# Side casts ahead of the sums' casts, an earlier rest for the weights' pieces, and two moved groups of transfers in a gated mix of linear and softmax attention

## The chip, the cores and the metric

The kernel runs on one core of a Trainium2 chip. The metric is the device time of one execution in microseconds. The kernel before took 2826.58 us as the median of three runs (2825.94 to 2827.85). The profiled execution, from which every row below comes, took 2824.52 us, 2.06 us under that median; its span of instructions is 2822.7 us.

## The reference

One token matrix `x` (2048 tokens, width 1024, fp32) goes through two attention blocks, and a gate mixes their outputs:

```python
x = A_x
g = _sigmoid((x * gate_w).sum(-1, keepdims=True))
a = _A_ref(x, A_wqkv, A_wo)     # linear attention, 32 heads of 32
b = _B_ref(x, B_wqkv, B_wo)     # softmax attention, 32 heads of 32
return g * a + (1 - g) * b

# in A: phi = lambda t: jnp.where(t > 0, t + 1, jnp.exp(t)) + 1e-6
#       o = phi(q) @ (phi(k)^T v) / (phi(q) @ sum(phi(k)) + 1e-6), then o @ wo
# in B: p = softmax(q k^T / sqrt(32)), then (p v) @ wo
```

## The kernel before

**Arithmetic.** [...] Where the result has to be near fp32, an operand is kept as two parts: `split` (line 293) makes `hi`, a ScalarE cast of the source, and `lo`, the source minus `hi`, on VectorE. `three` issues three matmuls for one product of such operands (lines 153, 156 and 158: hi with hi, hi with lo, lo with hi).

**Stages.** The program has one order for each engine, written out by hand (`manual_schedule`), and every engine works through its own order, waiting on semaphores.

1. A pass over the first half of the tokens for the values V (`v_pass(0, ...)`), to about 50 us of the span.
2. Eight *quads* of the first half (J=0). A quad makes two blocks of Q or K columns by a Strassen-like scheme with seven products instead of eight. `quad` runs `product(0)` to `product(6)`, 12 matmuls each, into the eight PSUM banks in turn (`bank[next(turns) % NQB]`). VectorE adds the products (the sums `C11`, `P1`, `W2`, `U2`), and `store` splits each finished sum and sends both parts to DRAM (`qk`).
3. `v_pass(1, ...)` for the second half: for each of eight steps it starts with all eight banks in order, so at its first step it needs every bank that the last quad used.
4. Eight quads of the second half (J=1), to about 415 us.
5. The long rest, from about 415 to 2675 us: linear attention (`linear`), the maxima of the softmax scores (`maxima`) and the heads (`heads_`) interleaved by a planner in the program (`T`, `use`, `behind`), which fixes the order when the program is built. Then the output product.

**Side work.** A quad has a generator `side`; each `next(side)` issues one step. `quad_weights` makes the seven weight operands of the next quad in six steps: adds and subtractions on VectorE, and splits (`part`) into a ring of 13 slots. The operand with number 2 is made in step 5 and is needed by the third product of the next quad. Also in `side`: `spill` stores the split x to DRAM, `reload_wv` loads V's weights again for the second half (transfers `big<-wv`), `change` (in the last quad of the first half) splits x of the second half, and `wo_parts` makes the operands of the output weights. The last runs on GpSimd: a piece is a cast, subtractions and transfers on GpSimd's own queue; a tiny ScalarE copy (line 511, `dn<-eps`) lets each piece start, and 28 pieces are spread over the steps of both halves.

**Transfers.** Nearly all transfers are issued by SyncE (line 170), in order. An issue also waits until the transfer eight issues earlier, which used the same semaphore, has landed.

**The long rest.** `load_half` loads half of a token's x (or of A's attention output) for `linear`; `store_mix` stores two or more small blocks of a mixed weight (`wa`). When a head's maxima are complete, `rows` turns them into a row, split into `mh` and `ml` (16 x 128 each), and four transfers write these into two extra rows of the head's query operand: token tiles 0 to 3 go to `q_first`, tiles 4 to 15 to `q_rest`. The matmul of line 1382 (scores of the head) reads `q_first` for j = 0 and `q_rest` for the others.

Of the kernel before, what the change touches and what calls it, by code (L numbers as in the profile page):

```python
# [3 lines left out]

# [16 lines left out]
DH = 32  # L21
C = 512
# [16 lines left out]
WARM = 8  # L39
NE = 3  # L40
AHEAD_X = 3
PIECE_STEP = 3.4
GATE_STEP, GATE_FROM = 2.3, 20.0
LATE = 1.0
MANUAL = {ET.PE, ET.DVE, ET.Activation, ET.SP, ET.Pool}
# [4 lines left out]
def kernel(  # L50
# [18 lines left out]
    nc = tc.nc  # L69
# [3 lines left out]
    HK = NK // 2  # L73
    NT = S // P
    NJ = S // C
    TPC = C // P
# [5 lines left out]
    def f32(ap):  # L82
        return ap.bitcast(F32)

    def f32r(ap):
        return ap.bitcast(F32R)
# [30 lines left out]
    mh = sb.tile([NT, P], F32R, name="mh")  # L117
    ml = sb.tile([NT, P], F32R, name="ml")
# [16 lines left out]
    q_first, q_rest = [big[0][:, :C], big[2][:, :C], None], [big[0], big[2]]  # L135
# [153 lines left out]
    def raw_tile(n):  # L289
        nraw[0] += 1  # L290
        return raws[nraw[0] % n]

    def split(hi, lo, src, eng):
        nc.scalar.copy(hi, src)  # L294
        eng.tensor_sub(lo, src, f32(hi))  # L295

    def load_cols(w, cols, k, n):

# [121 lines left out]
    def quad_weights(raws, J, f):  # L420

        w11, w12, w21, w22 = raws

        def part(s, raw):
            n = quad_ring(J, f, s)
            split(ring_w(n, 0), ring_w(n, 1), raw, nc.vector)

        part(0, w11)
        part(6, w22)
        nc.vector.tensor_add(w22, w21, w22)  # L430
        yield
        nc.vector.tensor_sub(w21, w11, w21)
        part(1, w12)
        yield
        nc.vector.tensor_sub(w11, w22, w11)
        part(3, w22)
        yield
        nc.vector.tensor_sub(w12, w12, w11)
        part(4, w11)
        yield  # L440
        part(2, w12)
        yield
        part(5, w21)
# [3 lines left out]
    def quad(J, f, side):  # L447

        sec, g = quad_cols(f)

        def product(s):
            ps = bank[next(turns) % NQB]
            n = quad_ring(J, f, s)
            for i in range(KH):
                sl = slice(i * P, (i + 1) * P)
                stat = [ring_w(n, p)[:, sl] for p in range(2)]
                for _ in three(ps, stat, [xpiece(J, PRODUCTS[s], p, i) for p in range(2)], i, n=KH):
                    pass
            return ps

        def store(i, jj, src, hi):
            split(f32r(hi), f32r(src), src, nc.vector)
            j = 2 * J + jj
            for p, part in enumerate((hi, src)):
                dma(qk_d[sec][p][g + i][:, j * C:(j + 1) * C], part)

        nc.scalar.copy(P1, product(0))
        next(side, None)
        nc.vector.tensor_add(C11, product(1), P1)
        store(0, 0, C11, H11)  # L470
        next(side, None)
        p3 = product(2)
        next(side, None)
        p5 = product(3)
        next(side, None)
        nc.vector.tensor_add(U2, product(4), P1)
        nc.vector.tensor_add(W2, p5, U2)
        nc.vector.tensor_add(P1, p3, W2)
        store(0, 1, P1, H12)
        next(side, None)  # L480
        p7 = product(5)
        nc.vector.tensor_add(W2, p7, W2)
        nc.vector.tensor_add(U2, p7, U2)
        store(1, 1, W2, H22)
        next(side, None)
        nc.vector.tensor_add(U2, product(6), U2)  # L486
        store(1, 0, U2, H21)
        next(side, None)

    def wo_piece(m, i):  # L490
        half, l = int(m[1]) - 1, int(m[2]) - 1
# [164 lines left out]
    def load_pair(raws, J, i):  # L656
        for k in (2 * i, 2 * i + 1):
            for jj in range(2):
                load_x(raws, J, jj, k)

    def quads(J, first, *others):

        sides_ = [late_side(J), *others]
        for f in range(QUADS - 1):
            if f + 2 < QUADS:
                load_quad(raws_q[f % 2], f + 2)
            else:
                first()
            quad(J, f, beside(quad_weights(raws_q[(f + 1) % 2], J, f + 1), *sides_))

    def spill_rest(J):
        part = 0
        for name in ("X11", "X21", "X22"):
            for _ in spill(J, name):
                part += 1
                for _ in range(2 if part % 4 else 1):
                    yield
# [50 lines left out]
        split_x(raw_x1[1], 1, 1, 3)  # L728
        yield

    quads(0, lambda: load_pair(raw_x1[0], 1, 0), reload_wv(), spill_rest(0), parts)
    load_pair(raw_x1[1], 1, 1)
    quad(0, QUADS - 1, change())
    for k in range(NK):
# [306 lines left out]
    def linear():  # L1041
        extra = iter(())
        for n, (i, t) in enumerate(units):
# [18 lines left out]
            for k in range(NK):  # L1062
                yield lambda: ended(w_left[k], w_ready[k], xp_ready.get(2 * n + k // HK, 0.0))
                need(w_left[k])
                if n < TPC:
                    stat = [xpiece(1, xname(0, k % 2), p, k // 2)[:, t * P:(t + 1) * P] for p in range(2)]
                else:
                    stat = [xstat_lin(n, k, p) for p in range(2)]
                for m, _ in enumerate(three(ps, stat, (wpart(k, 0), wpart(k, 1)), k)):
                    lin_pe(1.0)  # L1070
                    if m < 2:
                        yield always
                store_mix()
                if kind == "v":
                    if n in (4, 5) and k == 0:
                        load_v(n - 4)
                if n == 1 and k == 0:
                    for m in range(2 * TPC, 2 * TPC + 3):
                        load_half(m)
                if k % HK == HK - 1 and 2 * n + k // HK >= 2 * TPC:  # L1080
                    load_half(2 * n + k // HK + 3)
# [166 lines left out]
    def rows(h):  # L1248
        m = mneg
        end = use("dve", 0.14)  # L1250
        nc.vector.tensor_reduce(m, mx[h % 2], AX.X, ALU.max, negate=True)

        def turn():
            b = take()
            pm = bank[b]
            end = use("pe", 0.12, free[b])
            nc.tensor.transpose(pm[:NT, :P], m, ident)
            end = use("act", 0.2, end)
            nc.scalar.copy(mh, pm[:NT, :P])

            def low(end):
                rows_ready[h] = end + 2.5
                nc.vector.tensor_sub(ml, pm[:NT, :P], f32(mh))
                for i, part in enumerate((mh, ml)):
                    r = 3 * DH + i
                    for q, ts in ((q_first[h % 3], slice(0, TPC)), (q_rest[h % 2][:, C:], slice(TPC, NT))):
                        dma(f32(q[r:r + 1, :]).rearrange("o (t c) -> o t c", c=P), f32(part[ts]))

            give(b, 0.0, [defer(low, end, 0.2, 0)])

        tasks.append((lambda: both(bank_at(), end), turn))
# [654 lines left out]
```

## Time and profile before

| | |
|---|---|
| median of 3 runs | 2826.58 us |
| profiled execution, its time | 2824.52 us |
| its span of instructions | 2822.7 us |
| TensorE busy | 2801.9 us, 99% |
| VectorE busy | 2330.5 us, 83% |
| GpSimd busy | 2104.1 us, 75% |
| ScalarE busy | 1638.2 us, 58% |
| moved by transfers | 459.52 MB, mean 163 GB/s |

A row of a group or of the order of time names the line, the engine, the operation, what it writes and reads (`out<-in`, buffer numbers left out), the shape and the count; in brackets stands the idle time of the engine before it and what ended that. PE is TensorE, DVE VectorE, ACT ScalarE, POOL GpSimd, SP SyncE. A table of windows gives busy time (and count) of each engine in each stretch, TensorE's granted clock (PEclk), the busy share of the transfer engines and what they moved.

### The profile page before, as it was taken

The numbers are of one execution on the slowest core, as the hardware profiler recorded it, in microseconds if no ns is written. First come the engines' busy times: TensorE is split into PE (matmuls) and PEld (weight loads), VectorE is DVE, ScalarE is ACT, GpSimd is POOL, SyncE is SP. The second block draws the span as 40 slices with busy tenths as digits, with TensorE's granted clock in tenths as the row PEclk, the third lists the DMA queues.
The fourth block names the chain that finished last, engine by engine and source line by source line (L and its number), as shares of the span: only waits on it lengthen the run. The fifth ranks groups of instructions, "written<-read, shape, count | busy, mean of one in ns | idle before, by whom it ended". The sixth has DMA issues, their size and how long they took to land.

```text
span 2822.7 us, 47003 instructions
## 1 busy us (share of the span) xinstructions
PE 2801.9 (99%) x15880; PEld 2043.3 (72%) x15880; DVE 2330.5 (83%) x3745; ACT 1638.2 (58%) x3095; POOL 2104.1 (75%) x1150
## 2 busy tenths in 40 slices
PE   9999999999999999999999999999999999999999
PEld 8877887777767776677766777776676667666687
DVE  7887865888878888888888888888877888886688
ACT  5334332566666666666766666676666666666522
POOL 0651433699999999999899988989889988888000
PEclk9999999999999999999999999999999999999999
DMA  8997979533343434333433444456575555544774
GB/s 279 301 335 224 293 224 282 175 100 102 103 127 97 106 98 131 94 98 102 126 105 96 106 131 129 151 167 186 172 213 159 145 158 146 145 121 140 255 238 152
DMA packets 403340, 459.52 MB, mean 163 GB/s; under 512 B 106894, under 2 KB 234894, under 8 KB 401308
## 3 DMA queue, kind: packets, MB, share of 16 engines
q1 hardware_dynamic: 381084, 419.03, 47.5%
q0 software_dynamic: 22016, 37.50, 6.2%
q8 instruction: 126, 2.06, 0.3%
q14 instruction: 114, 0.93, 0.1%
HBM read 314.31 MB, written 127.66 MB: 157 GB/s over the span
## 4 chain that ended last, share of the span: by engine, by line
PE 90%; DMA 2%; issue 1%; DVE 0%; ACT 0%; SPq 0%; ACTq 0%; DVEq 0%
PE bank L1382 17%; PE bank L1240 16%; PE bank L1532 16%; PE bank L153 13%; PE bank L156 13%; PE bank L158 13%; PE bank L1304 1%; PE bank L1026 1%; PE bank L915 0%; DMA big<-ra 0%; DMA xh<-xs 0%; SPq L170 0%; PE bank L1296 0%; DMA qk<-mid 0%; DVE big L295 0%
## 5 line engine op out<-in xcount | busy, mean ns | idle before, releaser
L1467 POOL TENSOR_TENSOR big<-big,big 128x512 f32<-128x512 f32 (+2 forms) x694 | 1641.7, 2369 | 107.5 <-ACT big L1385 64.4
L1245 DVE TENSOR_REDUCE mx<-bank 128x1 f32<-128x512 f32 x2048 | 1313.5, 682 | 305.9 <-PE bank L1240 301.9
L1385 ACT ACTIVATE big<-bank 128x512 f32<-128x512 f32 x2048 | 1179.6, 602 | 433.7 <-PE bank L1382 368.4
L1382 PE MATMUL bank<-big,big 128*128 128x512 f32 x1888 | 742.4, 394 | 2.2 <-DMA big<-ml 2.2
L1240 PE MATMUL bank<-big,big 128*128 128x512 f32 x1888 | 739.8, 392 | 1.1 <-ACT big L1385 1.1
L153 PE MATMUL bank<-big,big 128*128 128x512 f32 x1576 | 618.1, 392 | 9.2 <-DVE mid L486 3.9
L158 PE MATMUL bank<-big,big 128*128 128x512 f32 x1572 | 614.9, 391 | 0.5 <-DMA big<-xs 0.2
L156 PE MATMUL bank<-big,big 128*128 128x512 f32 x1576 | 615.4, 390 | 0.0
L1532 PE MATMUL bank<-big,mid 128*32 128x512 f32 x4096 | 454.2, 593 | 0.0
L1382 PEld LDWEIGHTS bank<-big,big 128*128 128x128 f32 x1888 | 354.5, 188 | 127.3 <-issue 48.1
L1240 PEld LDWEIGHTS bank<-big,big 128*128 128x128 f32 x1888 | 355.0, 188 | 75.0 <-ACT big L1385 2.4
L153 PEld LDWEIGHTS bank<-big,big 128*128 128x128 f32 x1576 | 296.9, 188 | 77.6 <-ACT big L294 4.5
L158 PEld LDWEIGHTS bank<-big,big 128*128 128x128 f32 x1572 | 295.8, 188 | 65.9 <-DVE big L295 3.0
L156 PEld LDWEIGHTS bank<-big,big 128*128 128x128 f32 x1576 | 296.7, 188 | 61.3 <-DVE big L295 0.2
L1532 PEld LDWEIGHTS bank<-big,mid 128*32 128x32 f32 x4096 | 143.9, 110 | 264.1 <-issue 263.8
L1483 DVE TENSOR_TENSOR bank<-bank,big 128x512 f32<-128x512 f32 x364 | 251.5, 691 | 5.3 <-ACT big L1385 2.9
L295 DVE TENSOR_TENSOR big<-mid,big 128x512 fp32r<-128x512 f32 (+1 forms) x157 | 122.2, 795 | 44.6 <-ACT big L294 44.2
L294 ACT CAST big<-mid 128x512 fp32r<-128x512 f32 (+1 forms) x157 | 92.8, 618 | 113.1 <-DVE mid L1651 66.0
L1463 POOL TENSOR_TENSOR big<-big,big 128x1536 f32<-128x1536 f32 (+1 forms) x31 | 122.9, 3964 | 44.8 <-ACT big L1385 44.8
L153 PE MATMUL bank<-big,xh 128*128 128x512 f32 x376 | 147.1, 391 | 2.4 <-DMA xh<-xs 2.4
L158 PE MATMUL bank<-big,xh 128*128 128x512 f32 x376 | 146.9, 391 | 0.0
L156 PE MATMUL bank<-big,xh 128*128 128x512 f32 x376 | 146.8, 390 | 0.0
(163 smaller groups left out, 2123.0 us busy)
## 6 DMA issues: line engine op xcount, KB each, us to landing
big<-xs SPq DMA_DIRECT2D x288, 256.0 KB
big<-qk SPq DMA_DIRECT2D x690, 64.0 KB
xh<-xs SPq DMA_DIRECT2D x144, 256.0 KB
qk<-mid SPq DMA_DIRECT2D x128, 256.0 KB
big<-oA SPq DMA_DIRECT2D x84, 256.0 KB
xs<-big SPq DMA_DIRECT2D x64, 256.0 KB
oA<-mid SPq DMA_DIRECT2D x64, 256.0 KB
big<-big POOLq DMA_DIRECT2D x50, 256.0 KB, 5.4
```

The costliest lines, as they stand in the source:

```text
L153: yield nc.tensor.matmul(ps, sh, mh_, start=(kt == 0), stop=False)
L156: yield nc.tensor.matmul(ps, sh, ml_, start=False, stop=(late and last))
L158: yield nc.tensor.matmul(ps, sl, mh_, start=False, stop=last)
L295: eng.tensor_sub(lo, src, f32(hi))
L1240: nc.tensor.matmul(bank[b], q[:, t % TPC * P:(t % TPC + 1) * P], k[:, j * C:(j + 1) * C], start=True, stop=True)
L1245: nc.vector.tensor_reduce(m[:, t, j:j + 1], bank[b], AX.X, ALU.max)
L1382: nc.tensor.matmul(bank[b], k[:, t * P:(t + 1) * P], q_cols(h, j), start=True, stop=True)
L1385: nc.scalar.activation(pr_t[i][:, j * C:(j + 1) * C], bank[b], AF.Exp, scale=SCALE)
L1463: nc.gpsimd.tensor_add(lacc[:, :qp], pr(0)[:, :qp], pr(1)[:, :qp])
L1467: nc.gpsimd.tensor_add(lacc[:, sl], lacc[:, sl], pr(t)[:, sl])
L1483: nc.vector.tensor_add(lacc[:, qp:] if t == NT - 1 else l_b[:, :n], l_b[:, :n], src)
L1532: nc.tensor.matmul(av_b[j * DH:(j + 1) * DH, :], v[:, t, :], pr(t)[:, j * C:(j + 1) * C], start=(t == 0), stop=(t == NT - 1))
```

## The change

Four edits.

1. **Order in a quad.** `split` hands its VectorE part to `vec`. While `kept[0]` is a list, `vec` only notes the instruction. `step` runs one side step in that state: its ScalarE casts, GpSimd work and transfers are issued at once, its VectorE instructions are returned. `store` now issues the sum's cast, then the noted VectorE instructions, then the sum's subtraction. So in three places of a quad the side's casts stand ahead of the sum's cast on ScalarE, and the side's VectorE part stands between the sum and the sum's subtraction. The step that stood behind the store of `W2` is noted and issued only behind the last sum's addition (`U2 += product(6)`). Transfers of a side step (spills, reloads) now stand ahead of the sum's stores on SyncE.
2. **Rest of the pieces.** In the first half, `parts` advances for six quads (42 steps) instead of seven (49). In the order of instructions this makes 16 pieces in the first half and 12 in the second, where it was 19 and 9.
3. **`load_half` ahead of `store_mix`** in `linear`: x is issued before two blocks of `wa` instead of after them.
4. **Maxima's rows** go tile group by tile group: `mh` and `ml` of `q_first`, then `mh` and `ml` of `q_rest`; it was `mh` of both, then `ml` of both.

```diff
+    def vec(fn, *args):
+        if kept[0] is None:
+            fn(*args)
+        else:
+            kept[0].append((fn, args))
     def split(hi, lo, src, eng):
         nc.scalar.copy(hi, src)
-        eng.tensor_sub(lo, src, f32(hi))
+        if eng is nc.vector:
+            vec(eng.tensor_sub, lo, src, f32(hi))
+        else:
+            eng.tensor_sub(lo, src, f32(hi))
...
-        def store(i, jj, src, hi):
-            split(f32r(hi), f32r(src), src, nc.vector)
+        def step():
+            ops = kept[0] = []
+            next(side, None)
+            kept[0] = None
+            return ops
+
+        def store(i, jj, src, hi, ops=()):
+            nc.scalar.copy(f32r(hi), src)
+            for fn, args in ops:
+                fn(*args)
+            nc.vector.tensor_sub(f32r(src), src, hi)
...
-        store(0, 1, P1, H12)
-        next(side, None)
+        store(0, 1, P1, H12, ops)
         p7 = product(5)
+        ops = step()
         nc.vector.tensor_add(W2, p7, W2)
         nc.vector.tensor_add(U2, p7, U2)
         store(1, 1, W2, H22)
+        p4 = product(6)
         next(side, None)
-        nc.vector.tensor_add(U2, product(6), U2)
-        store(1, 0, U2, H21)
-        next(side, None)
+        nc.vector.tensor_add(U2, p4, U2)
+        store(1, 0, U2, H21, ops)
...
-    quads(0, lambda: load_pair(raw_x1[0], 1, 0), reload_wv(), spill_rest(0), parts)
+    quads(0, lambda: load_pair(raw_x1[0], 1, 0), reload_wv(), spill_rest(0), islice(parts, (QUADS - PIECE_REST) * NP))
...
+                if k % HK == HK - 1 and 2 * n + k // HK >= 2 * TPC:
+                    load_half(2 * n + k // HK + 3)
                 store_mix()
...
-                for i, part in enumerate((mh, ml)):
-                    r = 3 * DH + i
-                    for q, ts in ((q_first[h % 3], slice(0, TPC)), (q_rest[h % 2][:, C:], slice(TPC, NT))):
+                for q, ts in ((q_first[h % 3], slice(0, TPC)), (q_rest[h % 2][:, C:], slice(TPC, NT))):
+                    for i, part in enumerate((mh, ml)):
+                        r = 3 * DH + i
```

The order on TensorE and on GpSimd is the same in both kernels, instruction for instruction (line numbers aside).

**VectorE in the last quad of the first half**, from the first sum that reads `product(4)` (`bank_243`). `mid_234` is `U2`, `mid_235` `W2`, `mid_226` `P1`; `mid_231` to `mid_233` are the casts of the sums; `mid_224` to `mid_228` hold x of the second half, whose splits are the side work. Before:

```order
L476 TENSOR_TENSOR mid_234<-bank_243,mid_226 128x512
L477 TENSOR_TENSOR mid_235<-bank_242,mid_234 128x512
L478 TENSOR_TENSOR mid_226<-bank_241,mid_235 128x512
L295 TENSOR_TENSOR mid_226<-mid_226,mid_232 128x512
L295 TENSOR_TENSOR big_213<-mid_224,big_212 128x512
L295 TENSOR_TENSOR big_215<-mid_225,big_214 128x512
L482 TENSOR_TENSOR mid_235<-bank_244,mid_235 128x512
L483 TENSOR_TENSOR mid_234<-bank_244,mid_234 128x512
L295 TENSOR_TENSOR mid_235<-mid_235,mid_231 128x512
L295 TENSOR_TENSOR big_217<-mid_227,big_216 128x512
L295 TENSOR_TENSOR big_207<-mid_228,big_206 128x512
L486 TENSOR_TENSOR mid_234<-bank_245,mid_234 128x512
```

After:

```order
L499 TENSOR_TENSOR mid_234<-bank_243,mid_226 128x512
L500 TENSOR_TENSOR mid_235<-bank_242,mid_234 128x512
L501 TENSOR_TENSOR mid_226<-bank_241,mid_235 128x512
L481 TENSOR_TENSOR big_213<-mid_224,big_212 128x512
L481 TENSOR_TENSOR big_215<-mid_225,big_214 128x512
L482 TENSOR_TENSOR mid_226<-mid_226,mid_232 128x512
L505 TENSOR_TENSOR mid_235<-bank_244,mid_235 128x512
L506 TENSOR_TENSOR mid_234<-bank_244,mid_234 128x512
L482 TENSOR_TENSOR mid_235<-mid_235,mid_231 128x512
L510 TENSOR_TENSOR mid_234<-bank_245,mid_234 128x512
L481 TENSOR_TENSOR big_217<-mid_227,big_216 128x512
L481 TENSOR_TENSOR big_207<-mid_228,big_206 128x512
```

Two side subtractions moved ahead of `P1`'s own, and the addition that reads the last bank (`bank_245`) moved ahead of the other two.

**SyncE around the end of the seventh quad**, the stores of its last sums, the reloads of V's weights and the loads of x. Before:

```order
L170 DMA qk_0_7_135<-mid_231 128x512
L170 DMA qk_1_7_143<-mid_235 128x512
L170 DMA big_222<-wv_256 128x512 x2
L170 DMA qk_0_7_135<-mid_233 128x512
L170 DMA qk_1_7_143<-mid_234 128x512
L170 DMA big_223<-wv_257 128x512 x2
L170 DMA mid_224<-in_xT 128x512
L170 DMA mid_225<-in_xT 128x512
```

After:

```order
L170 DMA big_222<-wv_256 128x512 x2
L170 DMA qk_0_7_135<-mid_231 128x512
L170 DMA qk_1_7_143<-mid_235 128x512
L170 DMA big_223<-wv_257 128x512 x2
L170 DMA qk_0_7_135<-mid_233 128x512
L170 DMA qk_1_7_143<-mid_234 128x512
L170 DMA mid_224<-in_xT 128x512
L170 DMA mid_225<-in_xT 128x512
```

Each pair of stores now stands behind one pair of reloads more.

**SyncE near 2070 us**, a half of x, blocks of `wa` and a head's rows (`extra` is that head's `q_first`, `big_208` its `q_rest`). Before:

```order
L170 DMA wa_1_0_164<-big_4153 32x512 x2
L170 DMA xh<-xs_13_76 128x512
L170 DMA xh<-xs_13_92 128x512
L170 DMA wa_1_0_164<-big_4153 32x512 x2
L170 DMA extra<-mh 1x4x128
L170 DMA big_208<-mh 1x12x128
L170 DMA extra<-ml 1x4x128
L170 DMA big_208<-ml 1x12x128
```

After:

```order
L170 DMA xh<-xs_13_76 128x512
L170 DMA xh<-xs_13_92 128x512
L170 DMA wa_1_0_164<-big_4153 32x512 x4
L170 DMA extra<-mh 1x4x128
L170 DMA extra<-ml 1x4x128
L170 DMA big_208<-mh 1x12x128
L170 DMA big_208<-ml 1x12x128
```

The two transfers of x moved ahead of two of `wa`, and the `ml` row of `q_first` is the second of four instead of the third.

More of the change, by code (lines that the diff above doesn't have):

```diff
@@ L2 @@
 from contextlib import ExitStack
-from itertools import count
+from itertools import count, islice
 import concourse.bass as bass
@@ L41 @@
 AHEAD_X = 3
-PIECE_STEP = 3.4
+PIECE_STEP, PIECE_REST = 3.4, 2
 GATE_STEP, GATE_FROM = 2.3, 20.0
@@ L291, in raw_tile @@
         return raws[nraw[0] % n]
+    kept = [None]
+    def vec(fn, *args):
[3 more added lines that the diff above has]
+            kept[0].append((fn, args))
     def split(hi, lo, src, eng):
         nc.scalar.copy(hi, src)
-        eng.tensor_sub(lo, src, f32(hi))
+        if eng is nc.vector:
+            vec(eng.tensor_sub, lo, src, f32(hi))
+        else:
+            eng.tensor_sub(lo, src, f32(hi))
     def load_cols(w, cols, k, n):
@@ L429, in quad_weights @@
         part(6, w22)
-        nc.vector.tensor_add(w22, w21, w22)
+        vec(nc.vector.tensor_add, w22, w21, w22)
         yield
-        nc.vector.tensor_sub(w21, w11, w21)
+        vec(nc.vector.tensor_sub, w21, w11, w21)
         part(1, w12)
         yield
-        nc.vector.tensor_sub(w11, w22, w11)
+        vec(nc.vector.tensor_sub, w11, w22, w11)
         part(3, w22)
         yield
-        nc.vector.tensor_sub(w12, w12, w11)
+        vec(nc.vector.tensor_sub, w12, w12, w11)
         part(4, w11)
@@ L468, in quad @@
         next(side, None)
-        nc.vector.tensor_add(C11, product(1), P1)
-        store(0, 0, C11, H11)
-        next(side, None)
+        p2 = product(1)
+        ops = step()
+        nc.vector.tensor_add(C11, p2, P1)
+        store(0, 0, C11, H11, ops)
         p3 = product(2)
@@ L475, in quad @@
         next(side, None)
-        nc.vector.tensor_add(U2, product(4), P1)
+        p6 = product(4)
+        ops = step()
+        nc.vector.tensor_add(U2, p6, P1)
         nc.vector.tensor_add(W2, p5, U2)
         nc.vector.tensor_add(P1, p3, W2)
-        store(0, 1, P1, H12)
-        next(side, None)
+        store(0, 1, P1, H12, ops)
         p7 = product(5)
+        ops = step()
         nc.vector.tensor_add(W2, p7, W2)
@@ L484, in quad @@
         store(1, 1, W2, H22)
+        p4 = product(6)
         next(side, None)
-        nc.vector.tensor_add(U2, product(6), U2)
-        store(1, 0, U2, H21)
-        next(side, None)
+        nc.vector.tensor_add(U2, p4, U2)
+        store(1, 0, U2, H21, ops)
     def wo_piece(m, i):
@@ L1079, in linear @@
                         load_half(m)
-                if k % HK == HK - 1 and 2 * n + k // HK >= 2 * TPC:
-                    load_half(2 * n + k // HK + 3)
                 if k == 0 and n + 3 == len(units):
```

## The prediction

> **What bounds the kernel now.** I read the page first: who is busy.
>
> ```profile
> PE 2801.9 (99%) x15880; PEld 2043.3 (72%) x15880; DVE 2330.5 (83%) x3745; ACT 1638.2 (58%) x3095; POOL 2104.1 (75%) x1150
> ```
>
> TensorE is the bound, and its work and order do not change. So all that can be won is its own waits and slow clock. The view of waits, for TensorE alone (total, times, longest), names them:
>
> ```profile
> PE bank L153 <- DVE mid L486: 3.9, 1, 3.9
> PE bank L153 <- DMA xh<-xs: 2.4, 2, 1.7
> PE bank L153 <- ACT big L294: 2.3, 3, 1.2
> PE bank L1382 <- DMA big<-ml: 2.2, 2, 1.6
> ```
>
> Line 486 is a sum of a quad, line 294 a cast, `xh<-xs` is `load_half`, `big<-ml` a maxima row: each of the four edits has its wait here. The table of windows tells what these stretches lose (busy, count of matmuls, then the granted clock, the transfers' share and GB/s):
>
> ```profile
> 90.00:160.00 70.00, 69.49 (x303) 56.07 (x302) 61.07 (x77) 24.40 (x52) 46.97 (x64) 1.00 0.97 307
> 160.00:200.00 40.00, 39.10 (x172) 31.75 (x171) 34.30 (x44) 13.46 (x29) 22.71 (x31) 1.00 1.05 339
> 200.00:222.00 22.00, 16.23 (x58) 12.24 (x57) 19.02 (x25) 7.88 (x14) 8.54 (x11) 0.84 0.88 324
> 255.00:430.00 175.00, 175.00 (x774) 144.91 (x773) 122.70 (x177) 62.19 (x118) 68.72 (x97) 1.00 0.82 256
> 214.60:221.40 6.80, 5.45 (x13) 4.29 (x14) 5.97 (x11) 2.38 (x4) 0.40 (x1) 0.50 0.65 233
> ```
>
> The second half's quads (255 to 430) run without a gap: 774 matmuls in 175.0 us, one each 0.226 us. At that pace 90 to 160 misses 6.6 matmuls (1.5 us), 160 to 200 misses 4.9 (1.1 us), and 200 to 222 misses 39 (8.8 us): 11.4 us in the first half's quads and the start of the V pass behind them. Of the 8.8, the clock takes a part: from 215.95, where TensorE resumes, to 221.4 the clock is 0.50 and 13 matmuls run where 24 fit, so 2.5 us.
>
> **Edits 1 and 2, the last quad of the first half.** The order of time shows why the banks came free late. TensorE, VectorE, ScalarE and SyncE:
>
> ```profile
> 211.08 0.50 PE L153 MATMUL bank<-big,big 128*128 128x512 f32 x1 [1.49 <-DVE mid L483]
> 215.95 0.80 PE L153 MATMUL bank<-big,big 128*128 128x512 f32 x1 [3.90 <-DVE mid L486]
> ...
> 205.06 0.69 DVE L476 TENSOR_TENSOR mid<-bank,mid 128x512 f32<-128x512 f32 x1 [0.55 <-DMA qk<-mid]
> 207.93 0.69 DVE L295 TENSOR_TENSOR mid<-mid,mid 128x512 fp32r<-128x512 f32 x1 [0.73 <-ACT mid L294]
> 208.54 1.28 DVE L295 TENSOR_TENSOR big<-mid,big 128x512 fp32r<-128x512 f32 x2
> 209.75 0.68 DVE L482 TENSOR_TENSOR mid<-bank,mid 128x512 f32<-128x512 f32 x1
> 210.34 0.68 DVE L483 TENSOR_TENSOR mid<-bank,mid 128x512 f32<-128x512 f32 x1
> 212.27 3.03 DVE L295 TENSOR_TENSOR big<-mid,big 128x512 fp32r<-128x512 f32 x2
> 215.22 0.68 DVE L486 TENSOR_TENSOR mid<-bank,mid 128x512 f32<-128x512 f32 x1
> ...
> 207.80 1.13 ACT L294 CAST big<-mid 128x512 fp32r<-128x512 f32 x2
> ...
> 197.54 1.05 SPq L170 DMA_DIRECT2D qk<-mid  x2
> 200.56 3.45 SPq L170 DMA_DIRECT2D mid<-in_xT  x4
> ```
>
> The last bank is freed by line 486 at 215.90, behind two side subtractions that took 3.03 instead of the 1.28 of the same pair at 208.54. GpSimd works beside them; its rows, grouped over 186 to 216, and one of the list of transfers for the size:
>
> ```profile
> L514 POOL TENSOR_TENSOR big<-zrep,big 128x512 fp32r<-128x512 f32 x3 | 4.0, 1337 | 1.3 <-DMA woS<-big 1.3
> L516 POOL DMA_DIRECT2D woS<-big x4 | 2.2, 553 | 0.0
> L502 POOL DMA_DIRECT2D zrep<-in_b_wo x2 | 1.1, 564 | 0.6 <-POOL zrep L531 0.3 <-POOL zrep L537 0.3
> L516 POOL DMA_DIRECT2D woW<-big x2 | 1.1, 552 | 0.0
> zrep<-in_b_wo POOLq DMA_DIRECT2D x24, 256.0 KB, 5.8
> ```
>
> These are three pieces (L514 x3), just the three that edit 2 moves to the second half. With them go eight transfers of 256 KB, 2.1 MB in 30 us or 70 GB/s, 0.21 of the 339 and 324 GB/s of that stretch, whose transfer engines are full (share 1.05 and 0.88).
>
> Now I walk the new VectorE order with these durations. Its first sum (L476) waits for the store of the old `U2`, issued about 198.3 and landed 205.0, 6.7 us. In the new order that store stands behind one pair of reloads more, which speaks for no gain; the sum it stores is ready earlier, and the queue is shorter by 0.21, which speaks for 5.3 us. I take 5.3, since the transfers' share near 1 makes the wait a queue: the sum starts at 203.6 (bounds 205.06, as now, and no wait at all). Then, from the rows: three sums 2.14 (205.06 to 207.20, where the idle 0.73 before 207.93 begins), two side subtractions and `P1`'s own 0.6 apart, 1.8, with no idle 0.73 now; two sums 1.27 (209.75 to 211.02), which free the bank of line 483 at 208.8; the cast of `W2`, done about 0.1 later, `W2`'s subtraction 0.7, and at last line 486, 0.68, now ahead of the side's pair: 210.25 instead of 215.90, so 5.7 us.
>
> TensorE would ask for these banks earlier, because edit 1 also makes operand 2 earlier by the side's place ahead of `P1`'s cast: the 1.5 and 1.1 us before 200 go (three waits on ACT L294). That doesn't add to the 5.7: the end is set by line 486. It leaves waits before the banks of lines 478 (the third sum), 483 and 486 of about 1.1, 1.0 and 0.7 us, spread over 6 us, and I take it that the clock then stays at 1.00: 2.5 us more. Edits 1 and 2 together: **8.2 us**, between 4.2 (store as late as now, clock falls too) and 11.4 (no wait left).
>
> [...]
>
> ```profile
> 526.78 0.50 PE L1240 MATMUL bank<-big,big 128*128 128x512 f32 x1 [1.12 <-ACT big L1385]
> 528.60:532.00 3.40, 3.40 (x9) 2.62 (x9) 2.98 (x8) 1.94 (x4) 0.00 (x0) 0.51 0.56 187
> 2071.00:2075.00 4.00, 2.29 (x11) 1.61 (x10) 1.86 (x4) 2.85 (x6) 3.84 (x4) 1.00 0.49 148
> ```
>
> Here 1.12 us idle, followed by small matmuls, was followed by 3.4 us at 0.51 (9 matmuls for 15, 1.4 us), while 1.7 us idle near 2073 was not. By the first row the sum would be 1.4 lower; I stay with the second, the plainer case.
>
> What the moved pieces cost in the second half: cover there is TensorE's unbroken 175.00 us with nine pieces on GpSimd (68.72 us of POOL in all). Without that cover three pieces would cost what they do in 90 to 200, 2.6 us over about twelve pieces, so 0.7 us. I put them at nothing. The casts that now stand ahead of a sum's cast cost ScalarE 1.13 us per pair; it is busy 7.88 of 22 us there, and VectorE fills that time with the side's subtractions. The other fifteen quads gain VectorE time that nobody waits for, except as counted.
>
> **Edit 4, the rows.** In the chain of waits (start, duration, what):
>
> ```profile
> 2405.51 0.76 SPq L170
> 2406.37 2.31 DMA big<-ml
> 2595.82 0.76 SPq L170
> 2596.69 2.13 DMA big<-ml
> ```
>
> Line 1382 waits for the third transfer, `ml` of `q_first`; it now takes the second's place, 0.86 and 0.87 us earlier. The fourth lands as before, and the next matmul that needs it stands behind an attention block of some 7 us. The waits were 1.6 and 0.6 us (2.2 in all, longest 1.6), so 0.86 and 0.6: **1.5 us**. The 30 other heads don't wait, and don't gain.
>
> **Edit 3, x ahead of `wa`.** SyncE's order of time and the chain:
>
> ```profile
> 2068.62 0.88 SPq L170 DMA_DIRECT2D wa<-big  x2
> 2069.54 3.77 DMA xh<-xs
> ```
>
> The load is issued 0.92 us earlier, at 2068.62, of a wait of 1.7: **0.9 us**, up to 1.7 if the earlier mixes shift SyncE as well. The other xh wait (0.7) lies in the V chunk, where no `wa` is stored. `wa` itself is late by as much; it is read a chunk later.
>
> **Sum.** 8.2 + 1.5 + 0.9 = 10.6 us. 2824.52 - 10.6 = 2813.9 for a profiled execution; that one stands 2.06 under the median, so **2816.0 us** as a median, 0.38% faster. A measurement can tell about 0.2%, 5.65 us, from no change.
>
> **Rivals.**
>
> *Everything goes (0.18).* If the transfers' queue also runs ahead earlier, no store is waited for: 11.4 + 2.2 + 1.7 = 15.3, 2811.3 us. For it: the wait of L476 was only 0.55. Against it: the share is near 1 from 90 on, so the queue has no room to run ahead.
>
> *The store is the new wait, and the clock falls (0.17).* The old `U2` lands at 205.0 as now. All times of the walk move by 1.4, line 486 ends at 211.7, TensorE idles 2.5 before the first of the three banks and some 4.5 us in 8, and the clock halves: 4.2 + 2.4 = 6.6, 2820.0 us. For it: the reloads ahead of that store. [...]
>
> *The change does little in the quads (0.10).* If ScalarE's casts of x wait for their loads (issued 200.56, for 3.45 us, later in a longer queue), `P1`'s cast behind them is late, and so is every sum after. With loads that land at 210 line 486 ends near 215.9: only rows and x remain, about 2.4 to 5, 2822 to 2824 us. Against it: in the trace the casts at 207.80 did not wait for them.
>
> *Slower (0.05).* The stores of sums stand behind a side transfer in every quad. If that made each quad's first sum wait as L476 did, with two more issues of 0.65 us ahead, each of 15 quads would be late by up to 1.3 us: 19.5 - 10.6 = 9 us slower, 2835. It decides from 0.7 us a quad on. Against it:
>
> ```profile
> DVE mid L476 <- DMA qk<-mid: 0.5, 1, 0.5
> ```
>
> VectorE's waits between 50 and 420 us: that store was waited for once in sixteen quads.
>
> **Chances and range.** Forecast 0.50, with its own range 2813 to 2819 (the two bounds of the store's wait and the clock). The first rival lies below, the second reaches to 2821; all but a tenth of these two and the forecast are faster by over 0.2%: 0.83. The third rival and that tenth: 0.12 within 0.2%. Slower 0.05. The range takes in the first two rivals and the edge of the third: 2810.5 to 2822.
>
> **What would show it.** Right: matmul counts of about 309 in 90 to 160 and 177 in 160 to 200; the wait for the sum behind `product(6)` about 1 us instead of 3.9; no half clock there; rows' waits down to about 0.7; the xh wait down to 0.8. Wrong: a large wait of the first sum on `qk<-mid`, half clock near 210, casts of x waiting for `in_xT`, gaps in the second half's quads, or a new wait late in the program, where a shifted row or load meets another.

## The result and the profile after

The changed kernel takes 2808.13 us (median of 4 runs, 2805.40 to 2808.73) beside 2827.22 us of the kernel before (4 runs, 2825.94 to 2830.14): ratio 0.9929, 95% interval 0.9912 to 0.9946. The forecast was 10.6 us faster, 2816.0; it came out 19.1 us faster, below the range. The profiled execution took 2805.40 us. TensorE is now busy nearly all the time:

```profile
PE 2794.3 (100%) x15880; PEld 2040.4 (73%) x15880; DVE 2327.5 (83%) x3745; ACT 1640.2 (59%) x3095; POOL 2104.4 (75%) x1150
```

The table of windows of the changed kernel, for the stretches that were shown of before (busy and count of PE, PEld, DVE, ACT, POOL, then granted clock, the transfers' share, GB/s):

```profile
90.00:160.00 70.00, 70.00 (x311) 57.97 (x310) 62.75 (x83) 26.30 (x55) 41.33 (x55) 1.00 1.03 322
160.00:200.00 40.00, 40.00 (x178) 33.15 (x177) 29.23 (x39) 12.69 (x23) 19.84 (x28) 1.00 1.02 325
200.00:222.00 22.00, 20.93 (x92) 16.68 (x91) 19.71 (x32) 10.58 (x18) 0.00 (x0) 1.00 0.70 236
255.00:430.00 175.00, 174.67 (x771) 144.37 (x770) 124.36 (x173) 60.16 (x114) 82.24 (x115) 1.00 0.86 267
```

From 200 to 222 92 matmuls run where 58 did, at a granted clock of 1.00 (0.84 before). The waits of TensorE (total, times, longest), what is left but for three of 0.2 to 0.3 us:

```profile
PE bank L153 <- ACT big L302: 1.2, 1, 1.2
PE bank L650 <- DVE eps L110: 1.1, 1, 1.1
PE bank L153 <- DVE mid L506: 0.6, 1, 0.6
PE bank L153 <- DVE mx L1268: 0.6, 1, 0.6
PE bank L153 <- DVE mid L510: 0.5, 1, 0.5
```

Lines 506 and 510 are the sums that stood in lines 483 and 486. The order of time in the last quad of the first half, TensorE, VectorE and SyncE:

```profile
206.07 0.50 PE L153 MATMUL bank<-big,big 128*128 128x512 f32 x1 [0.61 <-DVE mid L506]
207.51 0.50 PE L153 MATMUL bank<-big,big 128*128 128x512 f32 x1 [0.46 <-DVE mid L510]
...
187.08 0.68 DVE L482 TENSOR_TENSOR mid<-mid,mid 128x512 fp32r<-128x512 f32 x1
...
198.91 0.69 DVE L499 TENSOR_TENSOR mid<-bank,mid 128x512 f32<-128x512 f32 x1 [2.56 <-DMA qk<-mid]
203.52 0.69 DVE L481 TENSOR_TENSOR big<-mid,big 128x512 fp32r<-128x512 f32 x1 [1.87 <-ACT big L302]
206.77 0.68 DVE L510 TENSOR_TENSOR mid<-bank,mid 128x512 f32<-128x512 f32 x1
...
190.69 1.79 SPq L170 DMA_DIRECT2D qk<-mid  x2
192.53 3.41 SPq L170 DMA_DIRECT2D mid<-in_xT  x4
```

VectorE finishes the old `U2` at 187.8 (it was 198.2, the row below), SyncE issues its store by 192.5 (it was 198.6, from 197.54 on), and VectorE, which was late before, now waits 2.56 us for that store.

```profile
197.55 0.69 DVE L295 TENSOR_TENSOR mid<-mid,mid 128x512 fp32r<-128x512 f32 x1 [0.73 <-ACT mid L294]
```

TensorE issues the same 15880 matmuls in the same order in every kernel here. So the time between the same two matmuls can be compared through all of them. The table gives it in us for the places where the executions differ; the head tells where that stretch lies in the trace before, and the last column adds the two rows of maxima (2405 to 2411 and 2596 to 2600).

```
                         70-185  185-223  223-309  436-458  514-537  2063-2079  rows
before                   115.15    37.89    86.13    21.51    22.97      15.88  10.65
before, again (e5)       116.80    38.31    86.13    20.99    21.24      15.87  10.04
edits 3+4 (e3)           121.03    38.65    86.13    20.71    21.43      13.92  10.05
edit 2 (e2)              115.25    34.78    86.13    19.67    21.13      17.61   9.62
casts ahead only (e7)    116.01    41.33    86.13    20.35    21.21      15.60   9.31
last quad only (e9)      122.30    29.68    87.20    21.23    23.07      13.94   8.48
edit 1 (e1)              113.33    28.21    89.27    21.66    20.84      14.00   9.80
edits 1+2 (e12)          113.33    29.03    86.13    21.35    20.92      15.11   9.79
without edit 4 (e10)     113.33    29.09    86.13    19.86    21.69      13.93   9.43
without edit 3 (e11)     113.33    27.20    86.13    20.78    21.62      14.96   8.96
after                    113.33    28.87    86.13    19.81    20.68      14.75   8.37
after, again (e6)        113.33    27.67    86.13    19.77    21.71      13.93   8.55
after, third (e12_after) 113.33    27.20    86.13    19.67    20.49      13.93   9.13
four quads rest (e8)     113.33    27.20    86.13    22.22    20.89      13.94   8.37
```

Two things are to be seen. With edit 1 the quads up to 185 take 113.33 us in each of eight executions; with the old order there they took 115.15 to 122.30, six different values. And the profiled execution from which the forecast was made is the lowest of these six in that stretch.

### The profile page after: what moved, and what is told of

Same layout as the page of the kernel before. It is cut to its first block, busy times and chain, and to the rows that moved or that the text cites. A ratio compares the mean times of both kernels' runs of the same rounds, so it can differ in the third digit from the quotient of the medians.

```text
span 2803.6 us, 46986 instructions
## 1 busy us (share of the span) xinstructions
PE 2794.3 (100%) x15880; PEld 2040.4 (73%) x15880; DVE 2327.5 (83%) x3745; ACT 1640.2 (59%) x3095; POOL 2104.4 (75%) x1150
## 3 DMA queue, kind: packets, MB, share of 16 engines
q8 instruction: 126, 2.06, 0.3%
## 4 chain that ended last, share of the span: by engine, by line
PE 91%; DMA 3%; DVE 1%; issue 1%; SPq 0%; ACT 0%; ACTq 0%; DVEq 0%
PE bank L1405 17%; PE bank L1263 17%; PE bank L1555 16%; PE bank L153 13%; PE bank L158 13%; PE bank L156 13%; PE bank L1327 1%; PE bank L1049 1%; DMA big<-wv 1%; SPq L170 0%; DMA big<-ra 0%; DMA xs<-big 0%; PE bank L938 0%; DMA mid<-in_xT 0%; DMA extra<-in_xT 0%
## 5 line engine op out<-in xcount | busy, mean ns | idle before, releaser
L1563 ACT COPY mid<-bank 128x512 f32<-128x512 f32 x32 | 18.8, 587 | 212.8 <-PE bank L1555 205.8
```

## The experiments

The theory of the forecast: the store of the old `U2` sets when the last quad's sums begin, and the length of the transfers' queue sets that store. The rival: VectorE's own lag sets it, and edit 1 takes the lag away. A third: GpSimd's pieces hold the first half. For the gains that nobody forecast (436 to 458 and 514 to 537): shift of the start, or chance.

### Each group of edits alone

Edit 1 alone (the new order, `parts` as before):

```diff
+        ops = step()
+        nc.vector.tensor_add(C11, p2, P1)
+        store(0, 0, C11, H11, ops)
...
     quads(0, ..., spill_rest(0), parts)
```

> Edit 1 alone (casts ahead, VectorE part behind; the last pieces still in the first half). If the transfers' queue sets when the old U2's store lands, as the prediction has it, the three pieces keep that queue full, the store lands at about 205 as before, line 486 ends near 211.7 and the clock still falls: the first half gains 4.2 us, at most 6.7. If instead VectorE's own lag sets when SyncE comes to that store (the rival), the order alone brings SyncE some 5 us ahead, no sum waits for a store, the half clock near 216 goes, and the first half gains 8 to 11 us. If the pieces are what matters, under 3 us. The stall at 526 and the waits at 440 to 453: they go if a shift of the program's start by some us takes them away, and stay if the other edits do.

Measured: 2810.97 us beside 2822.87 (ratio 0.9959, 0.9947 to 0.9971): 11.9 us by the medians. The first half is at 113.33 + 28.21: the rival holds. With all pieces in place TensorE has lost its stalls in the last quad but for one of 0.5 us, so the pieces alone did not set them. What makes the lag is in VectorE's waits between 100 and 225 us, first the kernel before:

```profile
DVE mid L295 <- ACT mid L294: 13.2, 18, 0.7
```

Eighteen times VectorE waited 0.73 us for the cast of a sum whose low part it was to make. In edit 1 alone that row is gone, and two others show VectorE ahead, waiting for products and for the store:

```profile
DVE mid L499 <- PE bank L158: 5.0, 3, 2.1
DVE mid L499 <- DMA qk<-mid: 2.3, 1, 2.3
```

This kernel lost 3.1 us behind the first half (89.27 for 86.13), in the only such loss of this size:

```profile
PE bank L153 <- ACT mid L369: 1.9, 1, 1.9
```

Line 369 copies V's results and waits there 2.7 us for a store of `v`. That the pieces, which edit 2 would have moved, put the work there late is likely, but argued from this one execution.

The pieces still cost VectorE time here. Beside a piece the side's pair of subtractions took 4.21 us, where 1.3 is usual, and it is 9.5 us from the first of the last quad's sums to the end of the last one (197.45 to 206.95):

```profile
199.51 4.21 DVE L481 TENSOR_TENSOR big<-mid,big 128x512 fp32r<-128x512 f32 x2
...
201.85 1.31 POOL L554 TENSOR_TENSOR zrep<-zrep 128x512 f32<-128x512 f32 x1
```

Edit 2 alone:

```diff
-    quads(0, ..., spill_rest(0), parts)
+    quads(0, ..., spill_rest(0), islice(parts, (QUADS - PIECE_REST) * NP))
```

> Edit 2 alone (two of seven... the last pieces moved behind the first half, old order of the side work). By the prediction: the pair of side subtractions ahead of line 486 takes 1.3 us instead of 3.0, and the store of the old U2 lands up to 1.4 us earlier, so line 486 ends 1.8 to 3.2 us earlier; the clock falls as before: 2 to 3 us in all, 5.6 if it does not fall. By the rival that VectorE's order sets it: under 2 us, and VectorE's wait order stays as it is. By the rival that GpSimd's work and transfers are the cause: most of the 10.9 us that the changed kernel gained up to 222.

Measured: 2820.03 us, 2.8 us less by the medians (0.9988, 0.9979 to 0.9997). The three waits of the last quad stay:

```profile
PE bank L153 <- DVE mid L478: 1.8, 1, 1.8
...
PE bank L153 <- DVE mid L486: 1.7, 1, 1.7
PE bank L153 <- DVE mid L483: 1.5, 1, 1.5
```

The wait for line 486 fell from 3.9 to 1.7, and the side's pair ahead of it took 1.29 us instead of 3.03, as the forecast had it. This varies without the edit too: the kernel before has 2.1 and 1.70 in the second execution below. But the old `U2`'s store was issued at 197.8 and landed at 204.9, 7.1 us; before it was 6.7. So it did not land sooner with the pieces' transfers gone. While that store was under way, the transfers' share and rate (the last two numbers) were, in the kernel before, with edit 2 alone and in the changed kernel:

```profile
198.30:205.00 6.70, 6.70 (x31) 5.55 (x30) 5.14 (x6) 2.50 (x5) 3.29 (x5) 1.00 1.03 331
...
197.80:204.90 7.10, 7.10 (x33) 5.89 (x32) 3.79 (x6) 3.26 (x6) 0.00 (x0) 1.00 0.96 350
...
192.10:198.80 6.70, 6.70 (x31) 5.53 (x31) 3.79 (x6) 2.48 (x5) 1.96 (x4) 1.00 1.05 386
```

The pieces' transfers are gone, but others moved as much or more.

Edits 1 and 2 together:

```diff
+        ops = step()
...
+    quads(0, ..., spill_rest(0), islice(parts, (QUADS - PIECE_REST) * NP))
```

> Edits 1 and 2 together. If the gains add up by stage, the first half gains 10.9 us as in the changed kernel, and the waits near 2073, 2408 and 2598 stay as before (3.3 us). If the gains of 1.7 us at 440 to 453 and 2.3 us at 526 to 532 come from the shift of the start, they are here too: 14.5 to 16 us in all. If they come from edit 3, which also places loads of x elsewhere, they are not: 11 to 12 us.

Measured: 2809.40 us (0.9951, 0.9939 to 0.9963), 13.5 us less, between the two expectations; the first half 142.36 for 153.04, and nothing lost behind it. Of the two gains that nobody forecast, the one at 514 to 537 is here (20.92) and the one at 436 to 458 is not (21.35). The waits near 2063 to 2079 and at the rows stay in part.

Edits 3 and 4:

```diff
+                if k % HK == HK - 1 and 2 * n + k // HK >= 2 * TPC:
+                    load_half(2 * n + k // HK + 3)
                 store_mix()
...
+                for q, ts in ((q_first[h % 3], slice(0, TPC)), (q_rest[h % 2][:, C:], slice(TPC, NT))):
+                    for i, part in enumerate((mh, ml)):
```

> Edits 3 and 4 alone (loads of x ahead of the mix's stores; rows tile by tile). By the prediction 0.9 + 1.5 = 2.4 us, with nothing elsewhere; by the changed kernel's trace 1.0 + 2.3 = 3.3 us. If edit 3 also takes the stalls at 440 to 453 and 526 away, 5 to 7 us. Nothing may change before 430 us.

Measured: 2821.61 us (0.9995, 0.9985 to 1.0004): no difference that the medians can tell. In the trace x gained all of its wait (13.92 for 15.88), and the first row, for once, nothing (1.7 us of wait in this execution). The 6.6 us more in the first half (121.03 + 38.65), where no instruction was changed, show how much the old order varies; this profiled execution lies 4.8 us above the median of its kernel.

### The same two kernels again

Nothing edited: the kernel before, and the changed one.

> The kernel before, unchanged, for a second profiled execution. Theory one: the waits of 1.1 us at 526 and of about 2 us at 440 to 453 belong to it and come again. Theory two: they are chance, and at least one of them is under 0.4 us here. [...]

Measured: 2823.91 us. The waits of TensorE include, by the waits' view,

```profile
PE bank L153 <- DVE mid L478: 2.5, 1, 2.5
...
PE bank L153 <- DVE mid L486: 2.1, 1, 2.1
...
PE bank L1240 <- ACT big L1385: 0.7, 1, 0.7
```

so the wait at 526 is 0.7 instead of 1.1 and the half clock behind it is missing; the waits at 428 to 460 come again, 1.7 us in sum (1.9 before). Neither theory holds to the letter. Two windows at half speed, at 216.9 to 223.7.

> The changed kernel, unchanged, for a second profiled execution. Theory one: no window at half speed before the end, line 1240's wait near 515 under 0.2 us and the waits between 428 and 445 under 1.2 us in sum, as in the first. Theory two (chance): one of the two places has a wait of 1 us or more, and the time is above 2807 us for that reason.

Measured: 2805.14 us. No window at half speed, but the wait that had seemed won at 526 is back:

```profile
PE bank L1263 <- ACT big L1408: 1.2, 1, 1.2
```

(line 1240 before). So theory two holds for that place, though not its time above 2807. Through the table: 514 to 537 takes 21.84 us in the mean of the six executions with the old order and 21.11 in the eight with the new; 436 to 458 takes 20.74 and 20.64. Of the 2.3 and 1.7 us that the first pair of traces showed there, 0.7 and 0.1 remain, less than executions differ by.

### What in edit 1 does it

Casts of the side's work ahead as in edit 1, their VectorE part at once instead of behind the sum (edits 2 to 4 left out):

```diff
         def step():
-            ops = kept[0] = []
-            next(side, None)
-            kept[0] = None
-            return ops
+            next(side, None)
+            return ()
```

> Edit 1 with the casts of the side work ahead as in it, but their VectorE part run at once, ahead of the sum, and not behind the sum's cast. VectorE then no longer waits for the side's casts (half of the 0.7 us waits), but waits for the cast of each sum as before, and a bank is freed later by the side's pair (1.3 us). If the gain comes from VectorE's smaller lag through both gaps, about half of what edit 1 alone gave remains (4 to 7 of 11.9 us). If it is only that casts no longer stand behind the sum's cast on ScalarE: 10 to 12 us. If it is the place of the VectorE part behind the sum: 0 to 3 us, and waits of TensorE on banks of sums appear throughout the quads.

Measured: 2824.68 beside 2824.75 us (1.0004, 0.9995 to 1.0013): nothing of 11.9 us. The third theory of this run holds for the time. The waits on banks of sums that it expected throughout the quads don't appear: up to 185 TensorE waits for casts (1.5 us), and the sums' banks hold it up in the last quad alone. VectorE's waits between 100 and 225 us, and its order of time in the last quad:

```profile
DVE mid L480 <- ACT mid L477: 13.2, 18, 0.7
```
```profile
212.25 0.69 DVE L297 TENSOR_TENSOR big<-mid,big 128x512 fp32r<-128x512 f32 x1 [2.59 <-ACT big L302]
214.31 0.75 DVE L297 TENSOR_TENSOR big<-mid,big 128x512 fp32r<-128x512 f32 x1 [1.36 <-ACT big L302]
...
216.42 0.69 DVE L499 TENSOR_TENSOR mid<-bank,mid 128x512 f32<-128x512 f32 x1
```

The eighteen waits are the same 13.2 us as before, since nothing stands between a sum's cast and its subtraction. And in the last quad the sums stand behind subtractions that wait 2.59 and 1.36 us for casts of x, so TensorE waits 9.1 us for line 499. What edit 1 gains comes from the place of the side's VectorE instructions: behind the sum they fill those 0.73 us, and the sum that frees a bank no longer stands behind them. These two effects of one move were not measured apart.

The new order in the last quad of each half alone, the seven quads ahead in the old one (edits 2 to 4 in place):

```diff
+        if f < QUADS - 1:
+            ...            # the old body, cast and subtraction together
+            return
         nc.scalar.copy(P1, product(0))
```

> The changed kernel with edit 1's order in the last quad of each half alone; the seven quads before keep the old order. If VectorE's lag builds up over the quads ahead (so that the old U2 is stored late), that store is issued near 197 and lands near 204, the walk of the prediction holds from there with that landing (second rival: line 510 ends at about 211), and the first half keeps 2.4 to 6 us of its 10.9; the waits before 200 stay as in the kernel before. If only the order inside the last quad matters, the first half keeps 10 us or more.

Measured: 2818.54 beside 2826.15 us (0.9969, 0.9958 to 0.9981), 7.6 us less. It splits the gain. VectorE's waits, its order of time and the windows:

```profile
DVE mid L482 <- ACT mid L479: 11.0, 15, 0.7
```
```profile
210.33 0.69 DVE L523 TENSOR_TENSOR mid<-bank,mid 128x512 f32<-128x512 f32 x1 [1.17 <-DMA qk<-mid]
...
216.79 0.68 DVE L534 TENSOR_TENSOR mid<-bank,mid 128x512 f32<-128x512 f32 x1
```
```profile
90.00:160.00 70.00, 65.92 (x280) 53.10 (x279) 62.40 (x72) 22.11 (x47) 46.41 (x61) 0.98 0.96 297
```

The quads up to 185 are as slow as any with the old order (280 matmuls for 311). From the first of the three sums (line 523) to the end of the last (line 534) it is 7.1 us, where the kernel before took 10.84 (205.06 to 215.90), and 185 to 223 takes 29.68 us, near the new kernel's 27.2 to 28.9. So both theories had a part: the order inside the last quad is worth most of that stretch even with a late store (issued at 204.1, landed at 210.2), the order of the quads ahead is worth the stretch up to 185 and the rest. By the medians of the runs taken side by side the order of the seven quads ahead is the larger part: 12.5 us (2818.54 against 2806.00 of the changed kernel below).

### Sizes of the smaller edits

Four quads' pieces left to the second half instead of two:

```diff
-PIECE_STEP, PIECE_REST = 3.4, 2
+PIECE_STEP, PIECE_REST = 3.4, 4
```

> The changed kernel with four quads' pieces left to the second half instead of two (PIECE_REST 4). If transfers and GpSimd's work of the pieces held the first half, it gains 0.5 to 2 us more there; if only the order of the work on VectorE mattered, nothing in the first half (its waits before 200 are gone already), and the second half, with six more pieces, stays without gaps or loses up to 1.5 us: within 0.1% of the changed kernel.

Measured: 2806.35 beside 2824.75 us (0.9930, 0.9917 to 0.9942). Nothing left to gain in the first half, and the second runs without a gap. It has a wait for x at 428 and the one half-speed window of the eight profiled executions with edit 1 throughout (waits, then windows):

```profile
PE bank L153 <- DMA xh<-xs: 2.2, 1, 2.2
```
```profile
427.24:430.65 3.41, 1.26 (x5) 1.00 (x6) 0.00 (x0) 0.72 (x1) 1.28 (x1) 1.00 0.99 305
430.65:434.06 3.41, 3.41 (x9) 2.65 (x8) 0.00 (x0) 0.12 (x1) 0.00 (x0) 0.50 1.15 301
```

The changed kernel without edit 4, without edit 3, and whole, on one chip:

```diff
-                for q, ts in (...q_first..., ...q_rest...):
-                    for i, part in enumerate((mh, ml)):
+                for i, part in enumerate((mh, ml)):
+                    for q, ts in (...q_first..., ...q_rest...):
```

> The changed kernel without edit 4. By the prediction 1.5 us slower than the changed kernel, by the waits of the runs so far 1.3 to 2.2 us, in waits before line 1405 at two places (0.7 to 1.6 and 0.2 to 0.6 us), and nothing else.

```diff
-                    load_half(2 * n + k // HK + 3)
                 store_mix()
...
+                    load_half(2 * n + k // HK + 3)
```

> The changed kernel without edit 3. By the prediction 0.9 us slower than the changed kernel, by the runs so far 1.0 to 1.7 us, in the wait for xh near 2056. If edit 3 also has a part in the waits at 428 to 445, these grow by about 1 us; otherwise they stay.

> The changed kernel, unchanged, beside the three others: 2805 to 2809 us; 14 us or more under the kernel before. Its waits at 428 to 445 and at 515 again differ by up to 1 us from its other executions, if they are chance; no window at half speed before 2600.

Measured: 2807.15, 2807.07 and 2806.00 us, with ranges that overlap, beside 2826.15; the whole kernel's ratio is 0.9929 (0.9917 to 0.9942), 20.2 us. The medians put 1.15 us on edit 4 and 1.07 on edit 3, which is not resolved by runs that spread over 3 to 4.5 us. By the table of stretches, seven executions with each edit against seven without: rows 8.84 against 9.81, so 1.0 us for edit 4; 14.05 against 15.58, so 1.5 us for edit 3 (1.2 if e2's, with its half-speed window, is left out; in e1 the wait for x is missing without edit 3). Edit 4 does not abolish the wait: it is 1.1 us in this execution of the whole kernel,

```profile
PE bank L1405 <- DMA big<-ml: 1.1, 2, 0.8
```

and 0 in the first. The stretch from 436 to 458 takes 20.78 us without edit 3 and 19.67 in this execution of the whole kernel, the 1 us that the expectation gave as a sign of edit 3. But SyncE's order is the same in both up to about 1945 us, where the first load of x moves, so this is scatter too.

## Why the prediction was off

- **Direction, place and mechanism of edit 1: right.** VectorE's sums freed the banks late, the side's pair stood ahead of line 486, and the new order cut the two stalls (3.90 and 1.49 us) to 0.46 and 0.61 and left the granted clock at 1.00 from 200 to 222 (0.84 before). 311 and 178 matmuls (about 309 and 177 forecast) from 90 to 160 and 160 to 200; the wait behind `product(6)` 0.46 us for "about 1".
- **The step that failed: "I take 5.3 ... the sum starts at 203.6".** It kept the issue of the old `U2`'s store at 198.3 and let it land sooner, since the queue would be shorter by the pieces' share. No run shows that a share near 1 makes the landing a queue that these transfers lengthen: while the store was under way the transfers moved 386 GB/s in the changed kernel and 331 before, and the landing took 6.8 us after, 7.1 with edit 2 alone, 6.7 before. The issue moved instead, by 6 us, since VectorE no longer lost 0.73 us eighteen times and finished that part 10.5 us earlier. The sum started at 198.91. From there the walk held in part: 6.65 us to the end of the last sum was forecast, and it was 6.6 in the second execution (199.84 to 206.43), 7.1 in e9 and 8.5 in the first, where it waits 1.87 us for a cast of x, the mechanism of the third rival. The other executions with edit 1 lie between 6.6 and 9.5.
- **"That doesn't add to the 5.7".** With a store fixed in time the waits before 200 could not add; with a store that moves along with the quads they do. In the same pair of executions 70 to 185 gained 1.8 us and 185 to 223 gained 9.0: 10.8 for 8.2. The 2.5 us for the half clock were in it, as forecast: that the clock would stay at 1.00 there was the author's estimate, and the trace after has it at 1.00 throughout that stretch.
- **"That one stands 2.06 under the median".** This was carried over as a constant, and the result does not fault it: the changed kernel's profiled execution stands 2.73 under its median, and the two profiled executions differ by 19.1 us, as the medians do. What the forecast did not see is how much the old order varies. The first half took 153.0 us in the execution that was priced, 155.1 in e5 and 159.7 in e3, mean 155.9. The three of the changed kernel took 142.2, 141.0 and 140.5, mean 141.2. By these means edits 1 and 2 gain 14.7 us, not 8.2; without e3's slow execution it is 12.8, and the medians of the run with edits 1 and 2 gave 13.5.
- **Edit 4:** 1.5 forecast, 1.0 in the mean. **Edit 3:** 0.9 forecast, 1.5 in the mean. Mechanisms as described; near 2073 no execution with edit 3 waits for x.
- **Nothing for the stall at 526 and the V chunk:** near the mean (0.7 and 0.1), but the first pair of traces showed 2.3 and 1.7 there. So of the 8.5 us that this pair gained beyond the forecast, 2.6 came from the first half, 0.8 from the rows, 0.2 from x, and 4.0, the largest part, from two stretches where mostly chance made the difference; 0.9 are spread over the rest.
- **The pieces at nothing:** right for the second half. What edit 2 buys was not foreseen: by the one execution without it, up to 3.1 us in the V pass behind the first half.

Sum of the means: 14.7 + 1.0 + 1.5 + 0.7 + 0.1 = 18.0 (16.1 without e3's first half); the medians of three comparisons gave 19.1, 19.6 (one run) and 20.2. Of the difference, 0.4 us lies between 537 and 2063 us in the mean; the rest, 1 to 4 us, stays open, and the scatter of the kernel before (2818.3 to 2827.9 in 23 runs) is large enough for it. The rival "everything goes" (2811.3) came nearest, and a part of its reason held: SyncE runs ahead earlier (the store's issue at 192.5 for 198.6), and the transfers' share of 1.03 and 1.02 (90 to 160 and 160 to 200) did not stand against it. Its condition, that no store is waited for, did not hold in two of three executions of the changed kernel (2.6 and 2.9 us of wait on VectorE, none in the third).

## What to carry to other kernels

When an engine's written order repeats "wait for a cast, then subtract" (here eighteen waits of 0.73 us), put independent work behind the cast, not ahead of the sum: moving the casts alone gained nothing here (2824.68 beside 2824.75 us). In a walk through a new order, move the issue times of everything that the faster engine triggers, its stores above all, before asking how long a transfer takes: here the store's issue moved by 6 us, and its landing took 6.8 us for 6.7. And price a change against several executions: where the removed waits vary, the one with a profile may be the best of them.

## What the runs showed of the hardware

**The granted clock behind the stalls.** In the trace before, the clock is at 0.50 in two stretches ahead of the last microseconds: from 214.61 to 221.44 us (6.83 us) and from 528.63 to 532.05 (3.41 us). Windows of 3.41 us there (of the 14 matmuls at 525.22, eight have one column):

```profile
211.20:214.61 3.41, 0.85 (x3) 0.36 (x3) 3.41 (x2) 0.97 (x2) 3.10 (x5) 1.00 1.06 408
...
525.22:528.63 3.41, 2.29 (x14) 1.73 (x14) 2.36 (x4) 2.15 (x5) 0.52 (x1) 1.00 0.31 108
528.63:532.05 3.42, 3.42 (x9) 2.64 (x9) 3.00 (x8) 1.91 (x4) 0.00 (x0) 0.50 0.55 183
2071.46:2074.88 3.42, 1.71 (x8) 1.24 (x7) 1.28 (x3) 2.48 (x5) 3.26 (x4) 1.00 0.43 129
```

After 525.22 (six of 512 columns) the clock is 0.50, after 2071.46 (eight) it stays at 1.00, though TensorE was idle for longer there (1.71 us for 1.12): this is what the forecast could not reconcile. In other traces such a window with three matmuls (e5, 213.49), five (e8, 427.24; e9, 133.70), six (e3, 112.30) and seven (e2, 2063.98) was followed by 0.50; in the trace before one with nine (2406.01) was followed by 1.00. What decides is not shown. A window at 0.50 in which TensorE did not wait held nine matmuls (528.63 to 532.05), where 15 fit at 0.226 us each: an estimate of 1.4 us lost.

The mean granted clock of the profiled execution is 0.998 or 0.999 in the six with the old order, 1.000 in seven of the eight with edit 1 throughout, and 0.999 in the eighth (e8). This may be a part of the old order's larger spread, which no run shows by itself.

**A store's latency at a transfers' share near 1.** With a share of 0.96 to 1.05 (the windows under "Edit 2 alone") the store of the old `U2` took 5.7 to 10.0 us from issue to landing: 6.7 and 8.9 in the kernel before, 6.8, 7.8 and 5.7 in the changed one, 7.0 with edit 1 alone, 7.1 with edit 2 alone and 10.0 without edit 4. Leaving out the pieces' 70 GB/s made no difference that stands out of this spread, and the rate while the store was under way did not fall: 331 and 371 GB/s in the kernel before, 386, 388 and 401 in the changed one.

**VectorE beside GpSimd.** In the first 420 us, 38 of the 255 subtractions that make a low part (128x512, VectorE) in the trace before ran for more than 0.3 us beside an addition or subtraction on GpSimd. These took 1.48 us in the mean and up to 2.46; the median of the others is 0.68. In the first trace of the changed kernel it was 33 of 255, 1.54 us and up to 2.46, beside 0.69.
